# Sliding-window attention, Fourier mixing and a feed-forward layer on one core: score tiles in bank e xor h, weight clamp before the shift, and six weight remainders on TensorE

## The chip, the core and the metric

The kernel runs on one NeuronCore of a Trainium2 chip. The metric is the device time of one execution in microseconds (us); lower is better. The core has a matrix engine (TensorE: PE for its multiplications, PEld for its weight loads), VectorE (DVE), ScalarE (ACT), GpSimd (POOL) and SyncE (SP, which only issues transfers here). Each engine works through its own instructions in order; semaphores tie them together.

## The reference

Attention with a mask per head, then a mixing layer by a two-dimensional Fourier transform, a normalisation and a two-matrix feed-forward layer, all in fp32 precision:

```
scores = scale * q @ k.T                      # 8 batches, 8 heads, 576 rows, head width 64
mask_plain = (rel >= 0) & (rel < 32)          # heads 0 to 3
mask_dil   = (rel >= 0) & (rel < 128) & (rel % 4 == 0)   # heads 4 to 7
x = softmax(where(mask, scores, -1e9)) @ v    # heads side by side: (8, 576, 512)
u = x + real(fft(fft(x, axis=1), axis=2))
un = (u - mean(u)) / sqrt(var(u) + 1e-6)
out = u + relu(un @ w_ch1) @ w_ch2            # 512 -> 2048 -> 512
```

The weights `w_ch1` and `w_ch2` come as 64-bit floats.

## The kernel before

**Attention.** A unit of attention (`attend`) is half of a pair of heads `e` = 0, 1: blocks of 64 queries against the 96 keys that their window can reach. One unit has 8 such blocks (`u` = 0) or 10 (`u` = 1, which takes the ninth block of both heads too); there are 64 units, 32 of them with `u` = 1. TensorE makes the scores (`score`, tiles of 64 by 64 of the array: head `e` lies on array rows 64e, output half `h` on PSUM partitions 64h). Before the change the tile of head `e` goes to PSUM bank `e`. DVE adds the mask and takes the row minimum of the negated scores (`masked`, one custom instruction and a short read of its accumulator), ACT takes the exponential, TensorE transposes (line 683), ACT copies (`ptsb`), TensorE multiplies with the values (`values`), DVE divides. The two ninth blocks lie in two banks, on 64 partitions each, so they are masked by two instructions of half height.

**Mixing.** `mix(b)` folds a batch (DVE or POOL), multiplies with cosine and sine tables along the sequence (`along_seq`, line 904) and along the channels (`along_channels`, line 950), adds (POOL) and normalises (DVE). Then a tile of 128 rows is transposed (`turned`) or read back from memory turned.

**Feed-forward in two parts.** Each fp32 operand is written as a high part in the matrix engine's reduced format and a remainder; three products of parts make one product. The first six blocks of the hidden width are computed while attention and mixing of later batches still run: `fill` is one such piece (72 multiplications of 256 columns, line 1080, then 36 of 512 columns, line 1096), 18 in all. The other ten blocks follow in a closing part (lines 1361, 1459, 1426) with fewer products. `narrow` turns 64-bit weights into fp32 by integer operations on DVE: a shift, two joins and a last step that multiplies a weight by 0 where its magnitude is below the smallest normal number (`F64_MIN`). `two_parts` makes the high part (ACT) and the remainder (a subtraction on POOL or DVE). `prep_up` and `prep` do this for the first six blocks of `w_ch1` (tiles `wa1`) and `w_ch2` (`wa2`), 512 columns each.

**What sets the order.** All operations go to a planner (`Plan`) with a cost and a priority. It simulates the engines and writes each engine's instructions in the order that it found. The constants `P_...`, `NSEQ`, `NCHN` and others near the top are priorities, and numbers of units after which tables are loaded. Where TensorE has nothing to do before the first `fill`, the planner puts in a pair of multiplications on a zero tile (`turn_over`, line 558, tile `blank`, which I call idle turns); from the first `fill` on it puts in none.

Of the kernel before, what the change touches and what calls it, by code (L numbers as in the profile page):

```python
# [39 lines left out]
NPT2, NAV2 = 13, 16  # L40
NGANG = 2
NU0, NU1 = 7, 9
NFD, NUD = 1, 0
PREPM = 1
P_QK0, P_V0 = -2.93, -6.43
P_ST, P_FD, P_WD, P_ST0, P_FD0, P_SPAN0, P_SPAN1 = -4.87, -7.33, -17.04, -48.63, -11.82, 2.3, 19.93
P_QK, P_V, P_TR, P_MIX, P_SPAN, P_W, P_WF, P_FILL, P_FILLT = -7.75, -5.61, -32.86, 8.4, 12.27, 26.16, 3.86, 38.57, 3.61
P_MIX0, P_MIX1 = -2.89, 6.05
NSEQ, NCHN = 5, 0
# [7 lines left out]
GAP = 64  # L57
# [7 lines left out]
F64_MIN = float(np.array([0x381 << 20], np.uint32).view(np.float32)[0])  # L65
# [136 lines left out]
PSUM_TAGS = ("sc", "sc1", "pt2", "av2", "pt", "av", "mix", "ff", "duo0", "duo1", "duo2")  # L202
# [196 lines left out]
def act(n):  # L399
    return n * 0.00083 + 0.1  # L400
# [29 lines left out]
def fused_kernel(ctx: ExitStack, tc, qk, v, w1, w2, seq, tail, chn, alt, mask, ident, perm, flip, out):  # L430
# [95 lines left out]
    blank = fixed(heads, [P, 2 * P], F32R, "blank")  # L526
# [14 lines left out]
    def start():  # L541
        dma(lambda: nc.sync.dma_start(out=mask_sb(), in_=mask), (), (mask_sb,), -7.9, P * 5 * KB * 4)
        dma(lambda: nc.sync.dma_start(out=ident_sb(), in_=ident), (), (ident_sb,), -7.8, P * 3 * P * 4)
# [5 lines left out]

        zero(half, "DVE", 0.07, lambda: nc.vector.memset(half(), -0.5))  # L550
# [4 lines left out]
        for n in range(NSPIN):  # L555
            def turn_over():
                for _ in range(2):
                    nc.tensor.matmul(spin()[:, :2 * P], lhsT=blank()[:, :P], rhs=blank(), start=True, stop=True)  # L558
            add("PE", 0.22, turn_over, (blank,), (spin,), SPIN, at=0.4 * n)
# [62 lines left out]
    def attend(b, dil, j, u, num, qk_, vt, xts, prio):  # L622
        slabs = [(((e, 2 * m), (e, 2 * m + 1)), (DIL_MASK if dil else PLAIN_MASK)[m], m)
# [34 lines left out]
        for i, (_, kind, _) in enumerate(slabs):  # L658
            for e in ((i % 2,) if i < 4 else range(2)):
                ps_ = slice(0, P) if i < 4 else slice(QB * e, QB * e + QB)  # L660

                def masked(i=i, kind=kind, e=e, ps_=ps_):
                    nc.vector.tensor_tensor_reduce(  # L663
                        prob(i)[ps_], sc()[e][ps_, KB * (i // 2):KB * (i // 2) + KB], mask_sb()[ps_, kind],
                        -0.125, 3.0e38, ALU.add, ALU.min, mx()[ps_, i:i + 1],
                    )
                add("DVE", 0.18, masked, (sc, mask_sb), (at(i), (mx, i)), prio)
# [338 lines left out]
    def narrow(rows, three, t, gate, prio):  # L1006
# [10 lines left out]
        def bits(dtype):  # L1017
# [16 lines left out]
        add("DVE", 0.6, lambda: nc.vector.scalar_tensor_tensor(  # L1034
            bits(F32), mag(), F64_MIN, bits(F32), op0=ALU.is_ge, op1=ALU.mult), (m,), (v,), prio)
        return lambda: shaped(bits(F32))

    def two_parts(src, need, dst, key, n, eng, prio):

        add("ACT", act(n), lambda: nc.scalar.copy(out=dst(0), in_=src()), need, ((key[0], (key[1], 0)),), prio)  # L1040
        lo = nc.gpsimd if eng == "POOL" else nc.vector
# [228 lines left out]
    for n in range(2 * NF1 + 1):  # L1270
# [3 lines left out]
        if n < 2 * NF1:  # L1274
            f, x = (n % NF1, n // NF1) if PREPM else divmod(n, 2)
            if x == 0:
                prep_up(f, wa1[f], utb(), (), P_W + P_WF * n / 2)
            else:
                prep(w2[P * f:P * f + P], False, wa2[f], utb(), (), P_W + P_WF * n / 2)
# [270 lines left out]
```

## Time and profile before

| | |
|---|---|
| timed runs, median (lowest to highest) | 1025.26 us (1023.63 to 1025.39) |
| profiled execution, its own time | 1022.32 us |
| span of its instructions | 1020.5 us |
| granted TensorE clock, mean | 1.000 |
| PE, DVE, ACT, POOL busy | 99%, 74%, 47%, 29% of the span |

The profiled execution spends 1.8 us outside the span of its instructions. It lies 2.9 us below the median of the timed runs. "Busy" of PE counts every stretch in which a multiplication is under way; idle turns and multiplications that lie between waits are in it.

### The profile page before, as it was taken

How to read it: one execution, taken by the hardware profiler on the slowest of the kernel's cores; microseconds unless marked ns; L12 is line 12 of the kernel's file. 1: busy time of each engine (PE TensorE's matmuls, PEld its weight loads, DVE VectorE, ACT ScalarE, POOL GpSimd, SP SyncE). 2: the span in 40 equal slices, each digit the busy share in tenths (PEclk: the TensorE clock that was granted, in tenths of full speed). 3: DMA queues.
4: the chain of work that ended last, by engine and by line, in shares of the span. 5: the costliest groups of instructions: out<-in, count | busy, mean ns of one | idle time of the engine just before them, and what ended most of it. 6: DMA issues, size and time to landing. Idle time of an engine off the chain costs nothing.

```text
span 1020.5 us, 22187 instructions
## 1 busy us (share of the span) xinstructions
PE 1006.4 (99%) x8347; PEld 898.2 (88%) x8347; DVE 750.4 (74%) x2203; ACT 479.4 (47%) x1186; POOL 291.4 (29%) x348
## 2 busy tenths in 40 slices
PE   9999999999999999999999999999999999999998
PEld 8788788888888888998988899999999989898987
DVE  4799967687867677686778876858585858585846
ACT  4776754464645444342445543535252525252522
POOL 2626454436243441846132510101010101010200
PEclk9999999999999999999999999999999999999999
DMA  9978765477656434432455232323232323232211
GB/s 313 305 240 252 220 199 175 146 209 212 197 151 195 120 118 135 150 105 93 132 169 155 84 83 83 84 83 83 83 84 83 83 84 83 83 84 83 83 62 42
DMA packets 99428, 138.49 MB, mean 136 GB/s; under 512 B 9838, under 2 KB 62619, under 8 KB 99321
## 3 DMA queue, kind: packets, MB, share of 16 engines
q1 hardware_dynamic: 94368, 126.10, 41.8%
q0 software_dynamic: 4032, 9.57, 3.2%
q8 instruction: 65, 1.06, 0.4%
q10 hardware_dynamic: 920, 1.41, 0.4%
q14 instruction: 43, 0.34, 0.1%
HBM read 99.24 MB, written 37.21 MB: 134 GB/s over the span
## 4 chain that ended last, share of the span: by engine, by line
PE 84%; DVE 8%; DMA 4%; issue 1%; ACT 1%; POOL 1%; ACTq 0%; SPq 0%; DVEq 0%; POOLq 0%
PE bank L1361 24%; PE bank L1459 20%; PE bank L1096 12%; PE bank L1080 11%; PE bank L950 3%; PE bank L696 3%; PE bank L683 3%; PE bank L632 2%; PE bank L558 2%; PE bank L904 2%; DMA ut<-in_w_dram 2%; PE bank L1426 1%; DVE pm L663 1%; DVE low L1088 1%; DMA ut<-us 1%
## 5 line engine op out<-in xcount | busy, mean ns | idle before, releaser
L1361 PE MATMUL bank<-low,wb 128*128 128x512 f32 x1080 | 255.9, 389 | 0.0
L1361 PEld LDWEIGHTS bank<-low,wb 128*128 128x128 f32 x1080 | 197.9, 188 | 37.4 <-ACT xb L1367 0.5
L1080 PE MATMUL bank<-ut,low 128*128 128x256 f32 x1296 | 168.0, 283 | 0.5 <-DVE low L1088 0.4
L1080 PEld LDWEIGHTS bank<-ut,low 128*128 128x128 f32 x1296 | 157.9, 189 | 3.7 <-DVE low L1088 1.5
L1096 PE MATMUL bank<-low 128*128 128x512 f32 x648 | 155.8, 393 | 0.0
L1124 POOL DMA_INDIRECT ut<-us,flip_sb x20 | 41.3, 2064 | 371.7 <-DVE ut L1181 243.1
L1096 PEld LDWEIGHTS bank<-low 128*128 128x128 f32 x648 | 118.7, 188 | 24.5 <-DVE low L1088 0.9
L1367 ACT ACTIVATE xa<-bank 128x256 f32<-128x256 f32 x90 | 34.2, 380 | 169.8 <-PE bank L1361 169.8
L669 ACT ACTIVATE pm<-pm,mx 128x96 f32<-128x96 f32 x256 | 83.7, 370 | 55.5 <-DVE mx L663 52.3
L1398 DVE TENSOR_TENSOR y<-xa 128x384 f32<-128x384 f32 x45 | 26.1, 581 | 95.5 <-ACT xa L1367 95.2
L1203 DVE STREAM_TRANSPOSE ut<-ut 128x512 f32<-128x512 f32 (+1 forms) x76 | 71.4, 977 | 11.4 <-DMA ut<-us 8.2
L1170 DVE TENSOR_TENSOR ut<-ut,bank 128x512 f32<-128x512 f32 (+1 forms) x136 | 73.1, 547 | 2.1
L1459 PEld LDWEIGHTS bank<-w2s,low 128*128 128x128 f32 x588 | 71.7, 188 | 2.1
L1459 PE MATMUL bank<-w2s,low 128*128 128x256 f32 x588 | 72.1, 278 | 0.0
L1086 ACT ACTIVATE low<-bank 128x256 fp32r<-128x256 f32 x108 | 41.2, 382 | 65.7 <-PE bank L1080 65.3
L1088 DVE SCALAR_TENSOR_TENSOR low<-bank,low 128x256 fp32r<-128x256 f32 x108 | 45.0, 419 | 31.4 <-ACT low L1086 30.5
L663 DVE CUSTOM_DVE_ANT_0 pm<-bank,mask_sb 128x96 f32<-128x96 f32 x256 | 55.5, 247 | 11.6 <-PE bank L632 10.4
L1459 PEld LDWEIGHTS bank<-w2s,hm 128*128 128x128 f32 x483 | 58.9, 188 | 1.8
L1459 PE MATMUL bank<-w2s,hm 128*128 128x256 f32 x483 | 59.2, 278 | 0.0
L1040 ACT CAST low<-y 128x640 fp32r<-128x640 f32 (+1 forms) x50 | 35.8, 717 | 40.0 <-DVE y L1400 24.8
L1116 ACT COPY row<-bank 128x512 f32<-128x512 f32 x36 | 21.0, 585 | 66.2 <-PE bank L1096 59.2
L1459 PE MATMUL bank<-low 128*128 128x256 f32 x420 | 51.5, 278 | 0.0
(182 smaller groups left out, 1833.5 us busy)
## 6 DMA issues: line engine op xcount, KB each, us to landing
qk<-in_qk_dram SPq DMA_DIRECT2D x30, 576.0 KB
vt<-in_v_dram SPq DMA_DIRECT2D x31, 438.8 KB
us<-uc SPq DMA_DIRECT2D x36, 257.0 KB
part<-row SPq DMA_DIRECT2D x36, 256.0 KB
wst<-in_w_dram SPq DMA_DIRECT2D x18, 512.0 KB
ut<-us SPq DMA_DIRECT2D x36, 256.0 KB
ut<-part SPq DMA_DIRECT2D x36, 256.0 KB
ut<-us SPq DMA_DIRECT2D x64, 128.0 KB
```

Source lines behind the costliest of these rows:

```text
L663: nc.vector.tensor_tensor_reduce(prob(i)[ps_], sc()[e][ps_, KB * (i // 2):KB * (i // 2) + KB], mask_sb()[ps_, kind], -0.125, 3.0e38, ALU.a ...
L669: add("ACT", 0.265, lambda i=i: nc.scalar.activation(out=prob(i), in_=prob(i), func=AF.Exp, bias=mx()[:, i:i + 1], scale=-1.0), ((mx, i),) ...
L1040: add("ACT", act(n), lambda: nc.scalar.copy(out=dst(0), in_=src()), need, ((key[0], (key[1], 0)),), prio)
L1080: nc.tensor.matmul(z()[:, :n_tok], lhsT=wf()[a][:, kk], rhs=ut()[:, p, kk], start=(kk == 0 and n == 0), stop=(kk == KT - 1 and n == 2),)
L1086: add("ACT", act(n_tok) - 0.05, lambda: nc.scalar.activation(out=h()[:, 0, :n_tok], in_=z()[:, :n_tok], func=AF.Relu), (z,), ((h, 0),), prio)
L1088: add("DVE", dve(n_tok), lambda: nc.vector.scalar_tensor_tensor(h()[:, 1, :n_tok], z()[:, :n_tok], 0.0, h()[:, 0, :n_tok].bitcast(F32), op ...
L1096: nc.tensor.matmul(acc(), lhsT=h()[:, a, P * s:P * s + P], rhs=wf()[:, p], start=(first and n == 0), stop=(last and n == 2),)
L1124: add("POOL", 1.04, lambda: nc.gpsimd.indirect_dma_start(dst(), None, us[idx // 4](), bass.IndirectOffsetOnAxis(ap=flip_sb()[:, 4 * kk + i ...
L1170: add("DVE", dve(C if at in (outer, inner) else TOK1), lambda: nc.vector.tensor_tensor(out=blocks(part())[:, at], in0=blocks(part())[:, at ...
L1203: nc.vector.transpose(out=o[back], in_=x[:, g])
L1361: nc.tensor.matmul(z(), lhsT=wb1[NF1 + 2 * p + f]()[:, a, kk], rhs=ut()[:, x, kk], start=(kk == 0 and n == 0), stop=(kk == KT - 1 and n == 2),
L1459: nc.tensor.matmul(acc()[block // 2][:, TOK1 * (block % 2):TOK1 * (block % 2) + TOK1], lhsT=part(hl, a, i, i + 1), rhs=w2s[p]()[:, j, x], ...
```

## The change

- **Scores:** the tile of head `e` and half `h` goes to bank `e ^ h`. A mask instruction of one bank then holds head `e` on one half and head `1 - e` on the other; `values` picks the matching half of the transposed tile. Both ninth blocks come to lie in bank 0, and one instruction of full height masks them.
- **Weights:** the magnitude is raised to `F64_LOW` first (a `max`, on a tile of 512 neighbouring words), and the exponent is shifted from that; the multiplication at the end is gone. The shift therefore waits for the ACT instruction that makes the magnitude.
- **Remainders of the six `wa1` tiles:** TensorE computes them as identity times the weights minus identity times their high part, in two halves of 256 columns, into a free part of bank 1 (`lo`); ACT copies each half out. The first of the two multiplications has fp32 operands. The other six (`wa2`) stay on POOL.
- **Planner:** other priorities; mask and identity tables are loaded through POOL's queue instead of SP's; the tables for `along_seq` are loaded after unit 1 (before: 5), those for `along_channels` after unit 8 (before: 0); bank pairs change over at unit 12 instead of 16.

```diff
-NPT2, NAV2 = 13, 16
+NPT2, NAV2 = 13, 12
+NLP = 6
-P_QK, P_V, P_TR, P_MIX, P_SPAN, P_W, P_WF, P_FILL, P_FILLT = -7.75, -5.61, -32.86, 8.4, 12.27, 26.16, 3.86, 38.57, 3.61
+P_QK, P_V, P_TR, P_MIX, P_SPAN, P_W, P_WF, P_FILL, P_FILLT = 5.65, -0.04, -32.59, 0.12, 12.45, 20.21, 4.61, 40.69, 3.61
-NSEQ, NCHN = 5, 0
+NSEQ, NCHN = 1, 8
...
-        slabs = [(((e, 2 * m), (e, 2 * m + 1)), (DIL_MASK if dil else PLAIN_MASK)[m], m)
+        slabs = [(((e, 2 * m), (1 - e, 2 * m + 1)), (DIL_MASK if dil else PLAIN_MASK)[m], m)
...
-                sc()[e][QB * h:QB * h + QB, KB * i:KB * i + KB], lhsT=qk_()[rows, GAP + S + QB * t:GAP + S + QB * t + QB],
+                sc()[e ^ h][QB * h:QB * h + QB, KB * i:KB * i + KB], lhsT=qk_()[rows, GAP + S + QB * t:GAP + S + QB * t + QB],
...
-            for e in ((i % 2,) if i < 4 else range(2)):
-                ps_ = slice(0, P) if i < 4 else slice(QB * e, QB * e + QB)
...
+                    prob(i), sc()[i % 2][:, KB * (i // 2):KB * (i // 2) + KB], mask_sb()[:, kind],
...
+        add("DVE", 0.34, lambda: nc.vector.tensor_scalar(mag(), mag(), F64_LOW, None, op0=ALU.max), (), (m,), prio)
         add("DVE", 0.34, lambda: nc.vector.tensor_scalar(
-            shaped(bits(U32)), words(1), 5, 2, op0=ALU.logical_shift_left, op1=ALU.logical_shift_right),
-            src, (v,), prio)
+            bits(U32), flat(t, 2 * C, C, U32), 5, 2, op0=ALU.logical_shift_left, op1=ALU.logical_shift_right),
+            (m,), (v,), prio)
...
-        add("DVE", 0.6, lambda: nc.vector.scalar_tensor_tensor(
-            bits(F32), mag(), F64_MIN, bits(F32), op0=ALU.is_ge, op1=ALU.mult), (m,), (v,), prio)
...
+        if eng == "PE":
...
+                    nc.tensor.matmul(ps(), lhsT=ident_sb()[:, 0], rhs=plain(src())[:, at], start=True, stop=False)
+                    nc.tensor.matmul(ps(), lhsT=neg(), rhs=plain(dst(0))[:, at], start=False, stop=True)
...
+                add("ACT", act(TOK1), lambda at=at, ps=ps: nc.scalar.copy(out=plain(dst(1))[:, at], in_=ps()),
...
-                prep_up(f, wa1[f], utb(), (), P_W + P_WF * n / 2)
+                prep_up(f, wa1[f], utb(), (), P_W + P_WF * n / 2, "PE" if n < NLP else "POOL")
```

The order of instructions, at three places.

TensorE at its start, before the change (`blank`: idle turns; `qk0`: scores of the first unit; the names at the left of the arrow are the PSUM banks written):

```order
L558 MATMUL bank7_142<-blank_161 128x256 x34
L632 MATMUL bank0_135<-qk0_158 64x96
L632 MATMUL bank1_136<-qk0_158 64x96
L632 MATMUL bank0_135<-qk0_158 64x96
L632 MATMUL bank1_136<-qk0_158 64x96
...
L558 MATMUL bank7_142<-blank_161 128x256 x8
```

and now:

```order
L562 MATMUL bank7_142<-blank_161 128x256 x42
L636 MATMUL bank0_135<-qk0_158 64x96
L636 MATMUL bank1_136<-qk0_158 64x96 x2
L636 MATMUL bank0_135<-qk0_158 64x96 x2
L636 MATMUL bank1_136<-qk0_158 64x96 x2
L636 MATMUL bank0_135<-qk0_158 64x96
L562 MATMUL bank7_142<-blank_161 128x256 x8
```

Eight idle turns more stand ahead of the first scores, and neighbouring score tiles now share a bank.

TensorE shortly before the first `fill` (L683 and L684: transposes; L696 and L699: values; L798 and L801: `turned`), before the change:

```order
L683 MATMUL bank2_137<-ident_sb_146,pm_1450 96x128 x2
L558 MATMUL bank7_142<-blank_161 128x256 x8
L683 MATMUL bank2_137<-perm_sb_147,pm_1517 96x128
L558 MATMUL bank7_142<-blank_161 128x256 x4
L683 MATMUL bank2_137<-perm_sb_147,pm_1517 96x128
L558 MATMUL bank7_142<-blank_161 128x256 x2
L683 MATMUL bank2_137<-ident_sb_146,pm_1517 96x128
L558 MATMUL bank7_142<-blank_161 128x256 x8
L696 MATMUL bank3_138<-vt_1209,ptsb_1532 64x65 x8
L798 MATMUL bank4_139<-ident_sb_146,uc_1544 128x128 x4
```

and now (L1050, L1051: the two multiplications of a remainder):

```order
L684 MATMUL bank2_137<-ident_sb_146,pm_1376 96x128 x3
L1050 MATMUL bank1_136<-ut_864,ident_sb_146 128x256
L1051 MATMUL bank1_136<-low_144,neg_162 128x256
L562 MATMUL bank7_142<-blank_161 128x256 x6
L684 MATMUL bank2_137<-perm_sb_147,pm_1454 96x128
L562 MATMUL bank7_142<-blank_161 128x256 x6
L1050 MATMUL bank1_136<-ut_887,ident_sb_146 128x256
L1051 MATMUL bank1_136<-low_144,neg_162 128x256
L684 MATMUL bank3_138<-ident_sb_146,pl_1330 96x128
L684 MATMUL bank2_137<-perm_sb_147,pm_1454 96x128
L562 MATMUL bank7_142<-blank_161 128x256 x6
L801 MATMUL bank4_139<-ident_sb_146,uc_1460 128x128 x4
```

Remainders stand where idle turns stood. Over the whole program 240 idle turns become 172, and 24 multiplications for remainders (12 of fp32, 12 of the reduced format) come in, 20 of them ahead of the first `fill`. That `fill` follows the same 188 score tiles in both orders. The last multiplication of `along_channels` stands ahead of the 15th `fill` before, ahead of the 12th now. From the first instruction of the closing part on, TensorE's 2955 instructions stand in the same order.

DVE at the masks of a unit with ninth blocks (ISA: the mask instruction), before the change:

```order
L663 ISA pm_865,mx_866<-bank1_136,mask_sb_145 128x96
L663 ISA mx_866 128x1
L708 RECIPROCAL rinv_883<-sums_876 128x5
L663 ISA pl_886,mx_866<-bank0_135,mask_sb_145 64x96
L663 ISA mx_866 64x1
L709 TENSOR_TENSOR xt_890<-bank6_141,rinv_883 128x4x64
L714 TENSOR_SCALAR xl_897<-bank6_141,rinv_883 128x64
L663 ISA pl_886,mx_866<-bank1_136,mask_sb_145 64x96
L663 ISA mx_866 64x1
```

and now:

```order
L664 ISA pm_725,mx_726<-bank1_136,mask_sb_145 128x96
L664 ISA mx_726 128x1
L709 TENSOR_SCALAR sums_736<-bank6_141 128x5
L664 ISA pl_738,mx_726<-bank0_135,mask_sb_145 128x96
L664 ISA mx_726 128x1
L711 RECIPROCAL rinv_744<-sums_736 128x5
```

One mask instruction takes the place of two. Ahead of the second low-part subtraction of `turned` (L806, now L809), which lets the first `fill` begin, DVE had 100 mask instructions and now has 90.

## Rows read from the trace of the kernel before

**Rows 1.** Page, parts 1 and 2: busy time; 40 slices in tenths.

```profile
PE 1006.4 (99%) x8347; PEld 898.2 (88%) x8347; DVE 750.4 (74%) x2203; ACT 479.4 (47%) x1186; POOL 291.4 (29%) x348
PE   9999999999999999999999999999999999999998
DVE  4799967687867677686778876858585858585846
```

**Rows 2.** Stretches: start:end, length, busy us of PE, PEld, DVE, ACT, POOL, clock, DMA.

```profile
0.00:86.40 86.40, 81.71 (x1129) 72.13 (x1130) 64.78 (x348) 53.23 (x150) 39.30 (x67) 1.00 0.94 286
86.40:552.00 465.60, 460.35 (x4266) 405.78 (x4265) 353.07 (x1240) 230.98 (x600) 198.11 (x250) 1.00 0.55 163
552.00:1016.40 464.40, 464.30 (x2955) 420.30 (x2953) 331.83 (x617) 195.23 (x438) 53.97 (x31) 1.00 0.28 80
...
50.00:86.40 36.40, 36.30 (x477) 32.35 (x470) 34.40 (x156) 24.62 (x68) 16.62 (x21) 1.00 0.84 253
```

**Rows 3.** TensorE in order of time: start us, us, what, count [idle before].

```profile
1.18 6.66 PE L558 MATMUL bank<-blank 128*128 128x256 f32 x34 [1.18 <-DVE blank L553]
7.77 0.56 PE L632 MATMUL bank<-qk 64*64 64x96 f32 x16
...
86.44 0.71 PE L1080 MATMUL bank<-ut,low 128*128 128x256 f32 x3
```

**Rows 4.** Chain that ended last, up to 90 us: start us, us, what.

```profile
32.38 1.19 PE bank L558 x10
33.58 0.62 PE bank L696 x16
34.20 0.49 PE bank L632 x16
```

**Rows 5.** Groups by shape, TensorE, whole span: operation, count, busy us, mean ns, idle.

```profile
L1361 PE MATMUL bank<-low,wb 128*128 128x512 f32 x1080 | 255.9, 389 | 0.0
L1080 PE MATMUL bank<-ut,low 128*128 128x256 f32 x1296 | 168.0, 283 | 0.5 <-DVE low L1088 0.4
L1096 PE MATMUL bank<-low 128*128 128x512 f32 x648 | 155.8, 393 | 0.0
L696 PE MATMUL bank<-vt,ptsb 96*64 96x65 f32 x1116 | 46.2, 227 | 1.2 <-ACT pm L669 0.9 <-ACT ptsb L685 0.2
L558 PE MATMUL bank<-blank 128*128 128x256 f32 x240 | 40.3, 311 | 1.2 <-DVE blank L553 1.2
L632 PE MATMUL bank<-qk 64*64 64x96 f32 x1116 | 40.3, 254 | 0.9 <-DVE mx L663 0.9
```

**Rows 6.** Groups by shape, DVE, 0 to 86.4 us.

```profile
L663 DVE CUSTOM_DVE_ANT_0 pl<-bank,mask_sb 64x96 f32<-64x96 f32 x20 | 5.0, 250 | 0.3
L1034 DVE SCALAR_TENSOR_TENSOR ut<-ut 128x512 f32<-128x512 f32 x5 | 3.6, 714 | 0.2
L1025 DVE TENSOR_SCALAR ut<-ut 128x512 uint32<-128x512 uint32 x6 | 3.5, 589 | 2.0 <-DMA ut<-in_w_dram 2.0
L709 DVE TENSOR_TENSOR xt<-bank,rinv 128x256 f32<-128x256 f32 x17 | 7.1, 420 | 0.6 <-DMA seq<-in_seq_dram 0.4
```

**Rows 7.** DVE in order of time, 41 to 47 us.

```profile
41.02 0.25 DVE L663 CUSTOM_DVE_ANT_0 pm<-bank,mask_sb 128x96 f32<-128x96 f32 x1
41.19 0.08 DVE L663 DVE_READ_ACCUMULATOR2_ANT mx<- 128x1 f32 x1
41.19 0.25 DVE L663 CUSTOM_DVE_ANT_0 pm<-bank,mask_sb 128x96 f32<-128x96 f32 x1
```

**Rows 8.** Groups by shape, ACT and POOL, 0 to 552 us.

```profile
L1086 ACT ACTIVATE low<-bank 128x256 fp32r<-128x256 f32 x108 | 41.2, 382 | 65.7 <-PE bank L1080 65.3
L1042 POOL TENSOR_TENSOR low<-ut,low 128x512 fp32r<-128x512 f32 x12 | 15.5, 1295 | 38.4 <-ACT low L1040 38.2
```

**Rows 9.** Whole chain that ended last: two undisturbed runs of a `fill`.

```profile
485.78 8.22 PE bank L1080 x72
494.00 8.26 PE bank L1096 x36
```

**Rows 10.** Waits of TensorE, whole span: total us, times, longest.

```profile
PE bank L683 <- ACT pm L669: 2.5, 4, 1.5
PE bank L683 <- ACT pl L669: 1.9, 2, 1.1
```

More of the change, by code (lines that the diff above doesn't have):

```diff
@@ L64 @@
 EPS = 1e-6
-F64_MIN = float(np.array([0x381 << 20], np.uint32).view(np.float32)[0])
+F64_LOW = 2.0 ** -15
 PASSES = ((0, 0), (1, 0), (0, 1))
@@ L525, in fused_kernel @@
     qks = [fixed(heads, [P, GAP + 2 * S], F32, f"qk{i}") for i in range(NQK)]
-    blank = fixed(heads, [P, 2 * P], F32R, "blank")
+    blank = fixed(heads, [P, P], F32R, "blank")
+    neg = fixed(heads, [P, P], F32R, "neg")
     xs = [fixed(keep, [P, C + 1], F32, f"x{i}") for i in range(NX)]
@@ L541, in start @@
     def start():
-        dma(lambda: nc.sync.dma_start(out=mask_sb(), in_=mask), (), (mask_sb,), -7.9, P * 5 * KB * 4)
-        dma(lambda: nc.sync.dma_start(out=ident_sb(), in_=ident), (), (ident_sb,), -7.8, P * 3 * P * 4)
+        add("POOL", 0.55, lambda: nc.gpsimd.dma_start(out=mask_sb(), in_=mask), (), (mask_sb,), -60.0, P * 5 * KB * 4)
+        add("POOL", 0.55, lambda: nc.gpsimd.dma_start(out=ident_sb(), in_=ident), (), (ident_sb,), -59.0, P * 3 * P * 4)
         dma(lambda: nc.sync.dma_start(out=perm_sb(), in_=perm), (), (perm_sb,), -7, P * 5 * P * 4)
@@ L548, in zero @@
             add(eng, cost, fn, (), ((t, key) if key is not None else t,), prio)
+        add("DVE", 0.2, lambda: nc.vector.tensor_scalar(neg(), ident_sb()[:, 0], -1.0, None, op0=ALU.mult), (ident_sb,), (neg,), -5.0)
         zero(half, "DVE", 0.07, lambda: nc.vector.memset(half(), -0.5))
@@ L557, in turn_over @@
                 for _ in range(2):
-                    nc.tensor.matmul(spin()[:, :2 * P], lhsT=blank()[:, :P], rhs=blank(), start=True, stop=True)
+                    nc.tensor.matmul(spin()[:, :2 * P], lhsT=blank(), rhs=blank().unsqueeze(1).broadcast_to([P, 2, P]), start=True, stop=True)
             add("PE", 0.22, turn_over, (blank,), (spin,), SPIN, at=0.4 * n)
@@ L658, in attend, with masked @@
         for i, (_, kind, _) in enumerate(slabs):
-            for e in ((i % 2,) if i < 4 else range(2)):
-                ps_ = slice(0, P) if i < 4 else slice(QB * e, QB * e + QB)
[L662 to L667, printed above, removed]
+            def masked(i=i, kind=kind):
+                nc.vector.tensor_tensor_reduce(
+                    prob(i), sc()[i % 2][:, KB * (i // 2):KB * (i // 2) + KB], mask_sb()[:, kind],
+                    -0.125, 3.0e38, ALU.add, ALU.min, mx()[:, i:i + 1],
+                )
+            add("DVE", 0.18, masked, (sc, mask_sb), (at(i), (mx, i)), prio)
         for i in range(n):
@@ L1040, in two_parts, with plain, go @@
         add("ACT", act(n), lambda: nc.scalar.copy(out=dst(0), in_=src()), need, ((key[0], (key[1], 0)),), prio)
+        if eng == "PE":
+            def plain(x):
+                return x.rearrange("p k f -> p (k f)") if len(x.shape) == 3 else x
+            for h in range(n // TOK1):
+                at, ps = slice(TOK1 * h, TOK1 * h + TOK1), bank("lo")
+                def go(at=at, ps=ps):
+                    nc.tensor.matmul(ps(), lhsT=ident_sb()[:, 0], rhs=plain(src())[:, at], start=True, stop=False)
+                    nc.tensor.matmul(ps(), lhsT=neg(), rhs=plain(dst(0))[:, at], start=False, stop=True)
+                add("PE", 2 * TOK1 / 1200 + pe(TOK1), go, (*need, (key[0], (key[1], 0)), ident_sb, neg), (ps,), prio)
+                add("ACT", act(TOK1), lambda at=at, ps=ps: nc.scalar.copy(out=plain(dst(1))[:, at], in_=ps()),
+                    (ps,), ((key[0], (key[1], 1)),), prio)
+            return
         lo = nc.gpsimd if eng == "POOL" else nc.vector
```

25 lines of the change are left out of this document (14 added, 11 removed).

## The prediction

> **What bounds the kernel now.** I read the page first: PE is busy for 99% of the span, DVE for 74% [rows 1]. A busy PE can still hold waits and idle turns, so I cut the span at two marks of the trace: the first multiplication of the first `fill` at 86.44 us [rows 3] and the start of the closing part at 552 us. The table of stretches then tells three stories [rows 2].
>
> From 552 us to 1016.40 us PE is busy for 464.30 of 464.40 us with 2955 multiplications. This is work without a gap, and the change leaves its order alone, so this stretch and the 4.1 us behind it keep their length. The term is 0.
>
> From 86.4 to 552 us PE is busy for 460.35 of 465.60 us. It stands idle for 5.3 us, but more is hidden. Two undisturbed pieces show what a `fill` costs at best: 72 multiplications in 8.22 us and 36 in 8.26 us [rows 9]. Eighteen of them are 148.0 and 148.7 us; the groups are busy for 168.0 and 155.8 us [rows 5]. Some 27 us are therefore spent where a `fill` is broken up by attention and mixing.
>
> Up to 86.4 us PE's 81.71 us contain 240 idle turns, 40.3 us of them busy [rows 2, 5]. This stretch isn't bound by PE's work. DVE is busy for 34.40 of the last 36.40 us ahead of the first `fill` [rows 2], so DVE sets the pace there, while in the first 50 us it idles for 50 - (64.78 - 34.40) = 19.6 us. Whatever brings the first `fill` forward brings the end forward, because the pieces behind it are packed.
>
> **The change, first stretch, by TensorE's queue.** The queue up to the first `fill` is packed, so I add and subtract.
> - Idle turns: the first 34 take 6.66 us, 0.196 us each [rows 3]. There are now 42: +1.6 us. Behind them stood 206, now 130: 76 fewer. Back to back one takes 0.119 us (ten in 1.19 us [rows 4]), that is -9.0 us; by busy time it is (40.3 - 6.7) / 206 = 0.163 us [rows 3, 5], that is -12.4 us.
> - Remainders: 10 of the 12 halves come ahead of the first `fill`. The trace has no fp32 multiplication of 256 columns on the whole array, so I build its cost. In the reduced format 256 columns more take 389 - 283 = 106 ns, 0.414 ns a column. For fp32, 96 columns take 254 ns and 65 take 227 ns, 0.87 ns a column, and one multiplication has two records (1116 here and 36 on a lent tile for 576 score tiles) [rows 5]. A half is 2 x 256 x 0.87 = 446 ns, plus 8.22 / 72 = 114 ns [rows 9], 0.56 us; ten are +5.6 us. Below: at 0.414 ns a column a half is 0.33 us, 3.3 us for ten. Above: with nothing overlapped, two records of 389 ns and one of 283 ns [rows 5], 1.06 us, 10.6 us for ten. I take 5.6, since the rows for fp32 are the nearer.
> - Eight multiplications with values move behind the first `fill` (the same 188 score tiles lie ahead): 16 records take 0.62 us [rows 4], -0.6 us.
>
> Sum: between -9.0 + 1.6 + 5.6 - 0.6 = -2.4 us and -12.4 + 1.6 + 5.6 - 0.6 = -5.8 us. I take -4.
>
> **The same stretch, by DVE.** Ten mask instructions fewer, at 41.19 - 41.02 = 0.17 us from one start to the next [rows 7]: -1.7 us. A mask instruction of half height isn't shorter (250 ns [rows 6]), so joining two saves a whole one. In `narrow` a join of 714 ns goes and a `max` comes, which I price as the other instruction with a constant, 589 ns [rows 6]; at the first `fill` the new order has done six tiles where the old one had done five last steps, so this is 6 x 0.589 - 5 x 0.714 = 0. Two divisions move behind: -0.8 us. Together -2.5 us by DVE's work alone. That is less than 4, but DVE has 19.6 us of idle time in its first 50 us, and the earlier start of mixing can use some. So -4 stands, and the bounds are -2 and -6.
>
> **Edits that I cost at nothing.** The POOL subtractions (1295 ns each [rows 8]) go for six tiles; POOL is busy for 39.30 of 86.40 us and nobody was shown waiting for it there. ACT gets 12 copies of 382 ns [rows 8], 4.6 us, and is busy for 53.23 of 86.40 us [rows 2]; its cover is gone only where a copy stands in front of an exponential (the second rival). Mask and identity loads stand first in POOL's order, ahead of its small clears; the first mask comes only behind 1.18 + 42 x 0.196 = 9.4 us of idle turns. The tables change places on POOL's queue. The clock is 1.00 in every stretch [rows 2], with no wait of PE over 1.5 us [rows 10]; shorter waits give it no reason to fall.
>
> **Middle stretch.** Two halves of remainders, +1.1 us, and the eight multiplications with values, +0.6 us. Against this DVE loses 22 mask instructions (3.7 us) and, for 26 tiles, 714 - 589 ns each (3.3 us), of 353.07 us. How much of the 27 hidden and 5.3 open us this and the new order give back, no row shows. Ends: a third of the 27 goes (-9), or the idle time doubles (+5.3). I take -3, nearer the middle, since DVE has 7 us less to do and mixing is through three pieces earlier.
>
> **Sum.** -4 + 1.7 - 3 = -5.3 us. The profiled execution's span goes from 1020.5 to 1015.2 us, its own time with the 1.8 us around it to 1017.0 us. It lay 2.9 us below the median of the timed runs, 1025.26 us, and that median is what is forecast: 1025.26 - 5.3 = **1020.0 us**. The likeliest case's own range is -5.8 + 1.7 - 9 to -2.4 + 1.7 + 5.3 at its ends, 1012 to 1030, mostly 1012 to 1025. A measurement of this kernel can tell about 0.2%, 2 us, from no change.
>
> **Rivals.**
> 1. *Row halves that share a bank stop overlapping; slower.* Sixteen records of scores take 0.49 us [rows 4], 31 ns each, while one of 96 columns streams for 96 x 0.87 = 84 ns: 2.7 stream at once. Until now the two heads, on different row halves of the array, wrote different banks; now the tiles of both write one bank, on different partitions. If at most two stream at once, a record takes 42 ns: 11 ns x 1152 records = +12.7 us, so -5.3 + 12.7 = +7.4, 1033 us. It decides from 5.3 / 1152 = 5 ns more a record. Against it: the value tiles, two halves of partitions in one bank, take 0.62 us for 16 records [rows 4], 39 ns for 65 x 0.87 = 57 ns of streaming, so partitions of one bank do overlap; but those tiles span all rows. The Trainium skill speaks against this change here (TensorEngine Tiling (Array Packing), Restrictions and Gotchas, Gotcha 1: PSUM Pressure): different row tiles write to different banks and cannot access the same bank simultaneously. By that rule the time is this rival's; by the rows on partitions it is the forecast. Chance 7%.
> 2. *The waits come back.* Six remainders now make TensorE's queue, and attention behind it, wait for DVE's words and ACT's high part, which nothing on PE waited for before the first `fill`. Waits behind ACT last (2.5 + 1.9) / 6 = 0.73 us in the mean, 1.5 us at most [rows 10]. Six of 0.73 are +4.4: 1024.4 us, no change; six of 1.5 are +9: 1029 us. For it: DVE has 2 us to spare in 36.40, and the transfer engines are busy at 0.94 up to the first `fill` [rows 2]. Against it: idle turns stand around the remainders in the order. Chance 20%.
> 3. *Mixing done sooner frees the fills.* If half of the 27 us goes: -4 + 1.7 - 13.5 = -15.8, 1009.5 us. For it: only 11 pieces instead of 14 lie among mixing. Against it: the same work must stand somewhere. Chance 12%.
> 4. *The change only moves work about* (fewer idle turns, the same waits as open idle time): then the remainders and values cost 1.7 us and the rest 0, 1027 us. Chance 6%.
>
> **How the numbers follow.** The forecast has 55%. Its own spread puts about 46 of these on faster, 6 on no change, 3 on slower. Rival 3 adds 12 to faster; rival 2 splits into 10 faster, 5 the same, 5 slower; rival 4 is 3 the same, 3 slower; rival 1 is 7 slower. Faster 0.68, same 0.14, slower 0.18. The range runs from 1010, rival 3, to 1028, past rival 4 and most of rival 2; what lies outside is rival 1 and the ends of the others, under 2 in 10.
>
> **What would show it.** In the new profile the first `fill` should begin near 82.4 us; 64.78 us of DVE work ahead of it should be about 62; a half of a remainder should take 0.56 us from its first start to the next instruction's; 16 score records should still take 0.49 us. From the first `fill` to the closing part there should be 464 us instead of 465.60, and the closing part 464.4 us. The prediction is wrong if the first `fill` doesn't come before 85 us, if PE shows waits for ACT's high parts (line 1042 of the new kernel) or for the copies of `lo`, if the score groups grow, or if the middle stretch grows by more than 4 us.

## The result and the profile after

| | before | after |
|---|---|---|
| timed runs, median (lowest to highest) | 1023.13 us (1021.33 to 1026.52) | 1030.05 us (1026.65 to 1035.71) |
| ratio to before, 95% interval | | 1.0071 (1.0054 to 1.0088) |
| profiled execution, its own time; span | 1022.32; 1020.5 us | 1029.38; 1027.3 us |

The change made the kernel 0.7% slower where 0.5% faster was forecast: +6.9 us for -5.3 us, and 1030.05 us lies above the forecast range of 1010 to 1028 us. The page after, parts 1 and 2 as in [rows 1]:

```profile
PE 1006.1 (98%) x8315; PEld 899.5 (88%) x8315; DVE 727.8 (71%) x2140; ACT 479.3 (47%) x1198; POOL 280.1 (27%) x344
PE   8879999999999999999999999999999999999998
PEclk9989999999999999999999999999999999999999
```

All engines have about as much work as before, or less; what is new is that PE isn't full in the first three slices and that its clock drops in the third. The table of stretches (columns as in [rows 2]), cut at the new first `fill` and at the closing part, says the same in numbers:

```profile
0.00:93.86 93.86, 81.95 (x1074) 70.86 (x1075) 58.27 (x325) 55.45 (x159) 33.90 (x64) 0.93 0.82 240
93.86:558.62 464.76, 459.89 (x4288) 408.02 (x4287) 348.35 (x1214) 231.18 (x605) 201.88 (x256) 1.00 0.58 171
558.62:1023.00 464.38, 464.24 (x2956) 420.56 (x2954) 320.56 (x603) 192.68 (x435) 44.31 (x25) 1.00 0.27 77
40.00:50.00 10.00, 8.57 (x117) 7.10 (x115) 2.95 (x22) 5.35 (x17) 7.63 (x15) 1.00 0.69 210
50.00:60.00 10.00, 3.19 (x43) 2.55 (x43) 5.05 (x22) 3.11 (x9) 3.61 (x7) 0.63 1.13 319
60.00:70.00 10.00, 10.00 (x115) 8.48 (x114) 7.83 (x38) 7.51 (x21) 0.00 (x0) 0.86 0.73 214
```

The second stretch takes 464.76 us (465.60 in [rows 2]), the closing part 464.38 us (464.40). The whole loss lies ahead of the first `fill`, which begins at 93.86 instead of 86.44 us [rows 3], and there between 40 and 75 us: the score tiles that PE begins at 43.19 us after the change, it began at 43.53 us before. The timelines of PE, DVE and ACT (start us, us, what, idle time before) show why:

```profile
43.19 0.73 PE L636 MATMUL bank<-qk 64*64 64x96 f32 x20
...
56.81 1.35 PE L699 MATMUL bank<-vt,ptsb 96*64 96x65 f32 x20 [7.54 <-ACT ptsb L690]
58.90 1.24 PE L636 MATMUL bank<-qk 64*64 64x96 f32 x20
...
54.17 0.43 DVE L856 TENSOR_TENSOR t<-x,x 128x257 f32<-128x257 f32 x1 [8.14 <-DMA x<-xsm]
...
55.71 0.41 ACT L874 CAST ees<-ee 128x257 fp32r<-128x257 f32 x1 [8.91 <-DVE ee L870]
```

DVE comes to the fold of batch 0 (line 856) at 46.0 us and stands there for 8.14 us, until the last input `x<-xsm` has landed. ACT's next instruction rounds the result of that fold and stands 8.91 us; the copy that PE waits for is queued behind it, so PE stands 7.54 us. In that idle time TensorE's granted clock falls to the lower of its two levels (1.2 and 2.4 GHz): it is 0.50 of full speed from 54 to 62 us, so that the two windows of 10 us show 0.63 and 0.86 in the mean, and 20 score records take 1.24 us at 58.90 where they took 0.73 us at 43.19.

Why is the input late? The timeline of POOL:

```profile
19.82 1.07 POOL L581 DMA_DIRECT2D seq<-in_seq_dram  x2
20.87 0.55 POOL L581 DMA_DIRECT2D tail_sb<-in_tail_dram  x1
21.40 1.07 POOL L581 DMA_DIRECT2D seq<-in_seq_dram  x2
22.79 0.59 POOL L540 DMA_DIRECT2D xsp<-xt  x1 [0.32 <-DVE mx L664]
23.37 1.06 POOL L540 DMA_DIRECT2D xsm<-xt  x2
29.19 0.70 POOL L540 DMA_DIRECT2D xsp<-xt  x1 [4.76 <-DMA seq<-in_seq_dram]
...
37.94 0.51 POOL L540 DMA_DIRECT2D xsm<-xt  x1 [1.75 <-DMA seq<-in_seq_dram]
...
46.75 0.57 POOL L540 DMA_DIRECT2D x<-xsm  x1
```

The five loads of the tables for `along_seq` stand ahead of batch 0's stores, and the stores wait for them to land. That is half of the story. The other half is an order: the fold stands behind 54 mask instructions on DVE, where it stood behind 71 before. Part of that is the joining of the ninth blocks; the rest is some two units of attention. The timelines of POOL and DVE before, and the view of that one transfer (its time to landing at the end), show the input and the fold (line 853):

```profile
46.42 0.54 POOL L537 DMA_DIRECT2D x<-ut  x1 [0.56 <-DMA seq<-in_seq_dram]
...
53.70 0.42 DVE L853 TENSOR_TENSOR t<-x,x 128x257 f32<-128x257 f32 x1
...
DMA to landing us min/median/max: 6.8/6.8/6.8
```

Before, the last input of the first fold landed at 46.42 + 6.8 = 53.2 us, and the fold came at 53.70 us without a wait. The chain that ended last shows the input and a table load after:

```profile
21.92 15.74 DMA seq<-in_seq_dram
...
46.75 7.39 DMA x<-xsm
```

There it landed at 46.75 + 7.39 = 54.14 us, only 0.9 us later than before; the fold was put 8 us ahead of it.

### The profile page after: what moved, and what is told of

Its sections match the earlier page's. It is cut to its first block, busy times and chain, and to the rows that moved or that the text cites. A ratio compares the mean times of both kernels' runs of the same rounds, so it can differ in the third digit from the quotient of the medians.

```text
span 1027.3 us, 22082 instructions
## 1 busy us (share of the span) xinstructions
PE 1006.1 (98%) x8315; PEld 899.5 (88%) x8315; DVE 727.8 (71%) x2140; ACT 479.3 (47%) x1198; POOL 280.1 (27%) x344
## 3 DMA queue, kind: packets, MB, share of 16 engines
q8 instruction: 65, 1.06, 0.4%
## 4 chain that ended last, share of the span: by engine, by line
PE 84%; DMA 6%; DVE 6%; ACT 2%; issue 1%; POOL 1%; SPq 0%; ACTq 0%; DVEq 0%; POOLq 0%
PE bank L1376 24%; PE bank L1474 20%; PE bank L1111 12%; PE bank L1095 12%; PE bank L953 3%; PE bank L907 3%; PE bank L699 3%; PE bank L636 2%; PE bank L684 2%; DMA us<-uc 2%; DMA seq<-in_seq_dram 2%; PE bank L1441 1%; DMA ident_sb<-in_ident_dram 1%; DMA x<-xsm 1%; DVE pm L664 1%
## 5 line engine op out<-in xcount | busy, mean ns | idle before, releaser
L1111 PE MATMUL bank<-low 128*128 128x512 f32 x648 | 153.2, 391 | 0.1
L699 PE MATMUL bank<-vt,ptsb 96*64 96x65 f32 x1116 | 46.7, 229 | 9.9 <-ACT ptsb L690 8.4
L699 PEld LDWEIGHTS bank<-vt,ptsb 96*64 96x64 f32 x1116 | 38.0, 139 | 20.2 <-ACT ptsb L690 9.7
```

Of the source, the lines that this page charges most:

```text
L699: nc.tensor.matmul(av()[QB * g:QB * g + QB, 65 * i:65 * i + 65], lhsT=pt()[:, at, QB * g:QB * g + QB], rhs=vt()[:, e, t], start=True, stop ...
L1111: nc.tensor.matmul(acc(), lhsT=h()[:, a, P * s:P * s + P], rhs=wf()[:, p], start=(first and n == 0), stop=(last and n == 2),)
```

## The experiments

The theories: 1, the tables ahead of the stores make the input late; 2, mask and identity tables through POOL's queue cost the start; 3, the edits of the computation cost the time; and, after the first four runs, 4, the fold's place. To move instructions and nothing else I left the plan alone and moved operations in the finished order, by a list for each kernel (what is moved, behind which operation; `MOVED` stands for the list of each kernel):

```diff
-        for o in order:
+        for o in moved(order):
             o.fn()
...
+def moved(order):
+    for what, behind, at in MOVED:
+        late = [o for o in order if o.tag == what]
+        rest = [o for o in order if o.tag != what]
+        k = [i for i, o in enumerate(rest) if o.tag == behind][at]
+        order = rest[:k + 1] + late + rest[k + 1:]
+    return order
```

Ratios go to the runs of before on the same chip; "fill" is the start of the first `fill` in the one profiled execution. For before_seq_early, before_fold_early and mask_sp that execution took 6.1, 3.1 and 2.7 us more than the median, so their "fill" is later than their ratio lets expect.

| kernel | median us | ratio (95%) | fill at us |
|---|---|---|---|
| before, after | 1023.13, 1030.05 | 1.0071 (1.0054 to 1.0088) | 86.44, 93.86 |
| seq_late | 1026.59 | 1.0027 (1.0013 to 1.0041) | 87.82 |
| both_late | 1024.36 | 1.0012 (0.9996 to 1.0027) | 90.41 |
| mask_sp | 1029.65 | 1.0054 (1.0040 to 1.0069) | 93.15 |
| before_seq_early | 1026.80 | 1.0027 (1.0014 to 1.0039) | 93.77 |
| fold_late | 1028.24 | 1.0058 (1.0041 to 1.0076) | 92.48 |
| before_fold_early | 1029.28 | 1.0062 (1.0047 to 1.0077) | 95.41 |
| fold_tables_late | 1019.78 | 0.9965 (0.9951 to 0.9979) | 84.74 |
| after_turns | 1026.43 | 1.0041 (1.0026 to 1.0055) | 91.87 |
| before_banks | 1024.17 | 0.9995 (0.9978 to 1.0012) | 86.27 |
| ft_half_turns | 1020.61 | 0.9958 (0.9942 to 0.9974) | 84.28 |
| ft_double_lo | 1025.36 | 1.0013 (0.9998 to 1.0029) | 89.52 |
| ft_mask_sp | 1021.42 | 0.9965 (0.9947 to 0.9982) | 83.20 |
| ft_again | 1021.14 | 0.9970 (0.9953 to 0.9987) | 83.61 |
| ft_lo_pool | 1022.05 | 0.9985 (0.9969 to 1.0000) | 86.88 |

**seq_late and both_late: after, with the tables moved.**

```diff
+MOVED = [("seq", "store", -1)]
...
+MOVED = [("seq", "store", -1), ("chn", "x1", -1)]
```

> The kernel after, with one thing moved: the five loads of the tables for along_seq stand on POOL's queue behind the last store of batch 0 instead of ahead of the first; every other instruction stands where it stood. Theory 1 (the tables ahead of the stores make batch 0's stores, its loads and so its fold late): the stores are issued without waits of 3 to 5 us, the fold of batch 0 no longer stands 8.1 us, PE's 7.5 us of idle time at 49 to 57 us shrinks below 2 us, the first fill begins at 84 to 87 us instead of 93.9, and the time falls by 6 to 9 us to 1021 to 1024, level with before. Theory 2 (mask and identity through POOL's queue cost the time, by a late first mask and a lower clock at the start) and theory 3 (the edits of the computation cost it): no change, 1029 to 1031. If what made the fold's inputs late is the traffic of the weight loads on SP's queue, the idle time shrinks by less than half and the time stays above 1026.

> As the run before, and the five loads of the tables for along_channels too stand behind the loads of batch 0's second row block on POOL's queue. Theory 1: if the tables for along_channels also slow the last input of the fold (7.4 us from issue to landing in the kernel after), 0.5 to 2 us better than the run before, 1020 to 1023; if they don't, level with it, and if along_channels comes to wait for its tables, up to 3 us worse. Theories 2 and 3: no change from the kernel after, 1029 to 1031.

DVE's timeline of seq_late:

```profile
44.54 0.43 DVE L856 TENSOR_TENSOR t<-x,x 128x257 f32<-128x257 f32 x1 [0.27 <-DMA x<-xsm]
...
56.35 0.43 DVE L856 TENSOR_TENSOR t<-x,x 128x257 f32<-128x257 f32 x1 [4.23 <-DMA x<-xsm]
```

and of both_late:

```profile
50.83 0.43 DVE L856 TENSOR_TENSOR t<-x,x 128x257 f32<-128x257 f32 x1 [7.31 <-DMA x<-xsm]
```

The tables cost 0.44 to 0.59% of the 0.71%: theory 1 holds in part. But the wait doesn't go away. In seq_late the first fold has its input 10 us earlier and the second stands 4.23 us, behind the tables for `along_channels`; in both_late the first stands 7.31 us again, earlier in time: its last input, issued at 42.80 us, is there only 8.0 us later, where that of seq_late, issued at 41.40 us, was there after 3.1 us. Why it took so much longer, no run shows. Behind each of these folds stands attention that needs nothing of it. That led to theory 4.

**mask_sp: after, with mask and identity through SP.**

```diff
-        add("POOL", 0.55, lambda: nc.gpsimd.dma_start(out=mask_sb(), in_=mask), (), (mask_sb,), -60.0, P * 5 * KB * 4)
+        add("POOL", 0.55, lambda: nc.sync.dma_start(out=mask_sb(), in_=mask), (), (mask_sb,), -60.0, P * 5 * KB * 4)
```

> The kernel after, with mask and identity tables loaded through SP's queue, first there; nothing else moved. Theory 2: the first mask comes 2 us earlier, the transposes of the first unit don't wait 1.55 us, the clock of 10 to 20 us returns from 0.83 to 1.00, and the time falls by 4 us or more, to 1026 or less. Theory 1: the start is 1 to 2 us earlier, but the stores still wait behind the tables and the fold's inputs come when they came, so the first fill begins at 93 to 94 us and the time is 1029 to 1031.

The start is some 2 us earlier, the clock of 10 to 20 us is 1.00 where it was 0.83, and DVE stands longer at the fold (9.60 us instead of 8.14). The ratio is 0.17% lower, within the intervals. Theory 2 falls as the cause.

**before_seq_early: the tables' turn alone, in before.**

```diff
+MOVED = [("chn", "x0", -1), ("seq", "store", 0)]
```

> The kernel before, with one thing moved, the other way round: the five loads of the tables for along_seq stand behind the first store of batch 0 on POOL's queue, as near as the kernel after has them, and those for along_channels behind the first loads of batch 0; no edit of the computation. Theory 1: stores wait for table loads, the fold of batch 0 waits 4 to 8 us, the first fill begins at 91 to 95 us instead of 86.4, and the time rises by 5 to 9 us to 1028 to 1032. Theories 2 and 3: within 1.5 us of before, 1022 to 1025.

Slower by 0.27%, about half of the least that theory 1 expected. The tables' turn costs without any edit of the computation, but not the whole loss, and not by the way expected: the first fold stands 1.62 us, not 4 to 8, and the longest wait of PE is 3.0 us.

**fold_late (in after) and before_fold_early (in before): the fold's place alone, both ways.**

```diff
+MOVED = [("fold0", "mask13", -1)]
...
+MOVED = [("fold0", "mask12", 0)]
```

> The kernel after, with one thing moved: the six DVE and two ACT instructions of batch 0's first fold stand two units of attention later, behind 63 mask instructions instead of 54 (before: 71); POOL's queue with its tables stays as it is. Theory 4 (the new order puts the fold ahead of work that doesn't need it, while its last input lands at 54.15 us, hardly later than the 53.3 us of before): DVE masks two units during the 8.1 us, PE's idle time of 7.5 us falls below 2.5 us, the clock stays at 1.00, the first fill begins at 85 to 88 us and the time is 1021 to 1025. Theory 1 (the tables ahead of the stores): what is late is the input, and the fold, the mixing behind it and the first fill stay late wherever the fold stands; the first fill begins at 91 us or later and the time is 1027 or more.

> The kernel before, with one thing moved: the eight instructions of batch 0's first fold stand some two units earlier on DVE and ACT; transfers, tables and the computation stay as they are. Theory 4: DVE stands 4 to 7 us for the fold's input, which lands at 53.3 us as before, PE gets an idle time of 3 to 6 us that before has not, the first fill begins at 90 to 94 us and the time rises by 4 to 8 us to 1027 to 1031. Theory 1 and theory 3 (the edits of the computation cost): within 2 us of before, 1021 to 1025, since the input comes no later and DVE makes up for the wait later.

DVE and PE of before_fold_early:

```profile
53.41 0.43 DVE L855 TENSOR_TENSOR t<-x,x 128x257 f32<-128x257 f32 x1 [3.84 <-DMA x<-ut]
...
55.77 1.35 PE L696 MATMUL bank<-vt,ptsb 96*64 96x65 f32 x20 [5.78 <-ACT ptsb L689]
...
95.41 0.72 PE L1080 MATMUL bank<-ut,low 128*128 128x256 f32 x3
```

Eight instructions moved by some two units make before 0.62% slower, with the same picture as after: DVE stands for the input, PE 5.78 us behind it. Theory 4 is shown in this direction. In the other it falls short: fold_late wins only 0.13%, within the intervals. PE's 7.54 us is gone there, but shorter waits stand in its place, as its timeline shows:

```profile
41.56 0.45 PE L684 MATMUL bank<-ident_sb,pm 128*96 128x128 f32 x1 [3.02 <-ACT pm L670]
...
61.40 0.31 PE L684 MATMUL bank<-ident_sb,pl 128*96 128x128 f32 x1 [1.73 <-DVE xt L712]
65.95 0.32 PE L684 MATMUL bank<-perm_sb,pm 128*96 128x128 f32 x1 [2.11 <-ACT pm L670]
```

and in its windows the clock is 0.66 from 40 to 50 us and 0.88 from 60 to 70 us. Stores that wait for the tables, and the second and third fold, which wait for inputs behind these stores, cost about what the first fold gave back, by these rows.

**fold_tables_late, and once more as ft_again: both moved, in after.**

```diff
+MOVED = [("seq", "store", -1), ("chn", "x2", -1), ("fold0", "mask13", -1)]
```

> The kernel after with both moved: the first fold two units later, the tables for along_seq behind the stores of batch 0 on POOL's queue, those for along_channels behind all loads of batch 0. Theories 1 and 4 together: PE has no idle time over 2 us before the first fill, which begins at 82 to 85 us as forecast, and the time is 1018 to 1021, 2 to 5 us below before; what the edits of the computation are worth then shows. If the first fill comes at 85 to 87 us with no idle time left, the sum for the first stretch (-4 us) was too hopeful, theory 3 holds in part, and the time is 1022 to 1024.

> The kernel with the fold later and both tables later once more, beside the run above on the same chip: ratio to before 0.995 to 0.998, first fill at 84 to 86 us. A ratio over 1.000 would make the gain of the two moves uncertain.

A window of fold_tables_late (columns as in [rows 2]):

```profile
50.00:60.00 10.00, 7.94 (x103) 6.22 (x103) 8.51 (x40) 6.79 (x21) 2.61 (x5) 1.00 1.08 284
```

and its timelines of DVE and PE:

```profile
52.31 0.43 DVE L856 TENSOR_TENSOR t<-x,x 128x257 f32<-128x257 f32 x1 [0.49 <-DMA x<-xsm]
...
54.03 1.41 PE L907 MATMUL bank<-seq,ees 128*128 128x290 f32 x6 [1.59 <-ACT ees L874]
...
84.74 1.23 PE L1095 MATMUL bank<-ut,low 128*128 128x256 f32 x9
```

No wait of PE over 2 us is left, the clock stays up, and the kernel is 0.35% faster than before (0.30% once more): 1.06% faster than after. One move alone gives 0.44 to 0.59%, the other 0.13%; together more than their sum, since either fault alone is enough to bring waits back. With both mended, theory 3 falls too: with all edits of the computation in it the kernel is faster than before. How much of this gain is the computation and how much the rest of the new order, no run separates; nor was before run with its own tables for `along_channels`, which stand ahead of batch 0's stores there, moved back.

**after_turns: after, with idle turns in the long wait.**

```diff
-        op = add("PE", 0.122 * n, values, (pt, vt), (av,), prio)
+        op = add("PE", 0.122 * n, lambda: ([nc.tensor.matmul(zs[1][:, :2 * P], lhsT=blank(), rhs=blank().unsqueeze(1).broadcast_to([P, 2, P]), start=True, stop=True) for _ in range(56 if num == 11 else 0)], values()), (pt, vt), (av,), prio)
```

> The kernel after, with 56 more idle turns on TensorE where it stands idle for 7.5 us, right ahead of the multiplication that waits (56 x 0.119 = 6.7 us of turns); they compute nothing that is used. If the granted clock that fell to half at 57 to 63 us is part of the loss, it stays at 1.00, 20 score records there take 0.73 instead of 1.24 us, the first fill begins 2 to 3 us earlier, at 91 to 92 us, and the time falls to 1027 to 1028. If the clock costs nothing because DVE sets the pace there, the time stays at 1029 to 1031.

Two windows of after_turns:

```profile
50.00:60.00 10.00, 8.80 (x99) 7.94 (x98) 6.07 (x30) 3.57 (x11) 4.81 (x9) 1.00 1.00 250
60.00:70.00 10.00, 9.62 (x119) 7.98 (x120) 8.53 (x40) 8.70 (x26) 0.00 (x0) 1.00 1.06 313
```

DVE still stands 8.25 us, but the clock is 1.00 where it was 0.63 and 0.86, and the time falls by 0.30%, 3 us. That is the part of the loss that the clock makes; the other 0.41% stays, and so does DVE's wait.

**before_banks: the score tiles alone, in before** (with the mask and the values following the tiles).

```diff
-                sc()[e][QB * h:QB * h + QB, KB * i:KB * i + KB], lhsT=qk_()[rows, GAP + S + QB * t:GAP + S + QB * t + QB],
+                sc()[e ^ h][QB * h:QB * h + QB, KB * i:KB * i + KB], lhsT=qk_()[rows, GAP + S + QB * t:GAP + S + QB * t + QB],
```

> The kernel before with the score tiles alone changed: head e, half h goes to bank e xor h, and the values pick the matching half; the ninth blocks still take two mask instructions, and every instruction stands where it stood. If row halves that share a bank stopped overlapping (rival 1 of the prediction), 16 score records would take 0.67 instead of 0.49 us and the time would rise by about 12 us to 1035. If they overlap as the kernel after shows, 16 records stay at 0.49 us and the time within 1.5 us of before, 1021 to 1024.

The chain of before_banks at its start:

```profile
7.80 0.49 PE bank L632 x16
```

No difference: rival 1 is out. Row halves that write one bank on different partitions stream at the rate that they had.

**ft_half_turns (the first edit) and ft_double_lo (the second): TensorE's queue, in fold_tables_late.**

```diff
-                for _ in range(2):
+                for _ in range(2 if n < 21 else 1):
...
-                    nc.tensor.matmul(ps(), lhsT=ident_sb()[:, 0], rhs=plain(src())[:, at], start=True, stop=False)
-                    nc.tensor.matmul(ps(), lhsT=neg(), rhs=plain(dst(0))[:, at], start=False, stop=True)
+                    for _ in range(2): nc.tensor.matmul(ps(), lhsT=ident_sb()[:, 0], rhs=plain(src())[:, at], start=True, stop=False), nc.tensor.matmul(ps(), lhsT=neg(), rhs=plain(dst(0))[:, at], start=False, stop=True)
```

> The kernel with the fold later and both tables later, with half of the idle turns left out behind the first scores (65 instead of 130). By the prediction's sum for TensorE's packed queue (0.119 us a turn) the first fill comes 7 to 8 us earlier, at 77 us, and the time falls to 1012. By DVE as the engine that sets the pace there, the first fill stays within 1.5 us of 84.7, PE shows as much more idle time as the turns took, and the time stays within 2 us of 1019.8; if the granted clock falls in these stretches, it rises to 1021 or more.

> The kernel with the fold later and both tables later, with the two multiplications of each remainder half made twice (the second pair writes the same values over the first). By TensorE's packed queue each half costs 0.56 us more, ten of them ahead of the first fill 5.6 us: first fill at 90 us, time 1025 to 1026. If the remainders lie in time that TensorE has over because DVE sets the pace, the first fill moves by less than 2 us and the time stays below 1022.

PE's timeline of ft_half_turns:

```profile
53.07 1.49 PE L907 MATMUL bank<-seq,ees 128*128 128x290 f32 x6 [2.26 <-ACT ees L874]
...
84.28 1.23 PE L1095 MATMUL bank<-ut,low 128*128 128x256 f32 x9
```

and of ft_double_lo:

```profile
89.52 1.23 PE L1095 MATMUL bank<-ut,low 128*128 128x256 f32 x9
```

65 idle turns fewer, 65 x 0.119 = 7.7 us by my sum, bring the first `fill` forward by 0.5 us: the turns fill waits and aren't on the path. (The clock is 0.83 from 50 to 60 us there, which takes some of the gain.) Ten remainder halves more put it back by 89.52 - 84.74 = 4.8 us, 0.48 us each: the remainders, which the work behind them waits for, are.

**ft_mask_sp: fold_tables_late with mask and identity through SP** (the edit of mask_sp).

> The kernel with the fold later and both tables later, and mask and identity tables first on SP's queue instead of POOL's. Theory 2 (a late start costs): the first units come up to 2 us earlier and, with no wait behind them to swallow it, the first fill too, at 83 us, time 1018. If the start is made up by 30 us anyway, as between before and after, the first fill stays within 0.7 us of 84.7 and the time within 1.5 us of 1019.8.

The first `fill` comes 1.5 us earlier than in fold_tables_late (0.4 us earlier than in ft_again), the ratio is the same. The better start isn't told from none.

**ft_lo_pool: the remainders back on POOL, in fold_tables_late.**

```diff
-                    nc.tensor.matmul(ps(), lhsT=ident_sb()[:, 0], rhs=plain(src())[:, at], start=True, stop=False)
-                    nc.tensor.matmul(ps(), lhsT=neg(), rhs=plain(dst(0))[:, at], start=False, stop=True)
...
-                add("ACT", act(TOK1), lambda at=at, ps=ps: nc.scalar.copy(out=plain(dst(1))[:, at], in_=ps()),
+                add("ACT", act(TOK1), lambda at=at, ps=ps: nc.gpsimd.tensor_tensor(out=plain(dst(1))[:, at], in0=plain(src())[:, at], in1=plain(dst(0))[:, at].bitcast(F32), op=ALU.subtract),
```

> The kernel with the fold later and both tables later, with the remainders of the six tiles made by POOL in halves, as a subtraction, instead of by TensorE and a copy of ACT; all other instructions stand where they stood. If the remainders are a term on the path (0.56 us each by the prediction, 4.8 us for ten by the run that doubles them), the first fill comes 3 to 6 us earlier, at 79 to 82 us, and the time falls to 1013 to 1017. If POOL's queue, with the loads of batch 0 in it, pays for the subtractions instead (12 of 0.7 us), the first fill stays within 1.5 us of 84.7 and the time at 1018 to 1021.

DVE and PE of ft_lo_pool:

```profile
52.02 0.43 DVE L856 TENSOR_TENSOR t<-x,x 128x257 f32<-128x257 f32 x1 [3.31 <-DMA x<-xsm]
...
53.74 2.04 PE L907 MATMUL bank<-seq,ees 128*128 128x290 f32 x6 [4.41 <-ACT ees L874]
```

The 5 us aren't given back: the subtractions stand between batch 0's loads on POOL's queue, the fold waits 3.31 us, PE 4.41 us, the clock is 0.54 from 50 to 60 us, and the ratio is no better (0.9985 against 0.9970, intervals that overlap).

## Why the prediction was wrong

**The step that failed** is "Edits that I cost at nothing", in its line that the tables change places on POOL's queue. I didn't name what stands behind them: batch 0's stores, then its loads, then the fold. And I didn't ask when the fold's input lands against where the new order puts the fold. Of the order I used only that "mixing is through three pieces earlier", as a gain. Both were there to be read before: the fold of before begins at 53.70 us, an input of it lands at 53.2 us, and the new order has 17 mask instructions fewer ahead of it. What the runs show in place of nothing: DVE waits 8.14 us for the fold's input and PE 7.54 us behind it, the first `fill` begins 7.4 us later instead of 4 us earlier, and moving the tables and the fold back takes 1.06% off the time. The mask and identity loads, in the same paragraph, weren't free either: the first mask stands on DVE behind the instruction that makes `neg`, which waits for the identity load until 10.29 us, and PE stands 1.55 us for it. But attention has made that up by 43 us, and mask_sp and ft_mask_sp show no gain clear of the intervals from mending it.

**The frame was right.** The first `fill` decides: +7.4 us there, +6.8 us in the span, and what lies behind takes its length (464.76 us, forecast 464; 464.38 us, forecast 464.4).

**TensorE's queue, -4 us.** The sum's two large terms are of different kinds. The remainders (+5.6 us) were sized well: 0.56 us each in the chain after, as forecast, and 0.48 us by the run that doubles them:

```profile
84.35 0.43 PE bank L1050 x2
84.78 0.13 PE bank L1051
```

The idle turns (-9.0 to -12.4 us) are hardly a term: half of them weigh 0.5 us. With the waits mended the first `fill` comes at 84.74 and 83.61 us, 1.7 and 2.8 us earlier than before, nearer to the -2.5 us that I had from DVE's work than to the queue's -4. So the rest of the change gains these 1.7 to 2.8 us and the 5 us that the remainders cost; which part of it gains how much, no run separates.

**DVE's work ahead of the first `fill`** is 58.27 us, forecast about 62. The masks and divisions came about as forecast: masks with their reads fall from 22.02 to 20.09 us (-1.9, forecast -1.7), divisions by 0.8 us. The term that was mis-sized is the weights, put at 0: their instructions fall from 16.0 to 13.5 us. I had priced the `max` by the old shift's 589 ns, but it takes 410 ns, and the shift itself, now on neighbouring words, takes 422 ns:

```profile
L1029 DVE TENSOR_SCALAR ut<-ut 128x512 uint32<-128x512 uint32 x6 | 2.5, 422 | 0.0
L1028 DVE TENSOR_SCALAR ut<-ut 128x512 f32<-128x512 f32 x6 | 2.5, 410 | 0.0
```

The last 1.3 us of the 6.5 are spread over small instructions.

**Middle stretch, -1.3 us:** measured -0.8 us. **Clock:** "shorter waits give it no reason to fall" failed twice. A long wait came, of 7.54 us, and the clock that fell behind it cost 3 us. And short waits were no safeguard: the clock was 0.83 from 10 to 20 us behind a wait of 1.55 us, and 0.83 from 50 to 60 us of ft_half_turns behind one of 2.26 us. The rows of the kernel after:

```profile
10.00:20.00 10.00, 8.85 (x125) 7.79 (x126) 4.54 (x37) 5.20 (x17) 0.31 (x2) 0.83 1.04 301
...
11.15 0.31 PE L684 MATMUL bank<-perm_sb,pm 128*96 128x128 f32 x1 [1.55 <-ACT pm L670]
```

**Rivals.** Rival 1 is shown wrong (16 records in 0.49 us, before_banks). By the rule of the Trainium skill (TensorEngine Tiling (Array Packing), Restrictions and Gotchas, Gotcha 1: PSUM Pressure) that different row tiles cannot access one bank simultaneously, the scores should have slowed; the measurement decides, and on different partitions of one bank they didn't. Rival 2 had the right kind, waits that come back behind DVE and ACT, but in the wrong place: behind the fold, not behind the remainders; that its upper price, 1029 us, lies near the 1030.05 measured is luck. With both faults mended the kernel takes 0.9965 and 0.9970 of before, -3.6 and -3.1 us against the forecast -5.3, but that is another kernel than the one forecast.

## What to carry to other kernels

When an order changes, look first not for what became shorter but for every instruction that waits for a transfer: read in the old trace when its input landed, and count how much work the new order leaves ahead of it on its engine. An in-order engine that comes to such an instruction early stops everything behind it, needed or not, and two engines further the matrix engine pays with its clock as well. Transfers that gate a chain (store, load, fold) want to stand ahead of bulk loads on their queue, even if those are needed soon.

## What the hardware showed that I had not expected

A transfer on POOL's queue in this kernel is issued only when the one eight places earlier has landed, as far as the rows show. In the rows above the fifth load of tables is issued at 21.92 us and lands 15.74 us later, at 37.66 us; the store eight places behind it is issued at 37.94 us, after a wait for `seq`. In the kernel before, the load issued at 45.32 us has waited 1.11 us for that of `tail_sb`, eight places ahead of it. Whether the queue or the program's semaphores make it so, no run here shows. So here a bulk load holds back the issue of the transfers behind it. And idle turns in the long wait are worth 3 us, though they compute nothing: with them TensorE's clock is 1.00 when the wait is over, without them 0.50.
